# Four batches, all first-layer weights and two second-layer loads in transfers of 2 MB

## The chip, the cores and the metric

One core of a Trainium2 chip runs the whole kernel. The metric is the device time of one execution in microseconds (us). TensorE (PE) multiplies, VectorE (DVE), ScalarE (ACT) and GpSimd (POOL) do the rest, and SyncE (SP) issues nearly all transfers between HBM and on-chip memory. A transfer is cut into packets, one for each row that is contiguous on both sides, and they are spread over the core's 16 DMA engines. In this text 1 MB of a transfer is 1024 KB, that is 128 partitions of 8 KB.

## The reference

The inputs are `x` (8 batches, 8 heads, 512 tokens, 64), `state` (8, 8, 32, 64), and a soft mixture of 8 experts with 4 slots each (`phi`, `w1` 8x512x1024, `w2` 8x1024x512), all float32:

```
scores = x @ state.T / 8 ; a = softmax(scores) ; xread = a @ state
scores2 = state @ x.T / 8 ; a2 = softmax(scores2) ; sread = a2 @ x
X = concat(xread, sread) per batch, heads side by side      # 4608 x 512
logits = X @ phi
slot_input = softmax(logits, over tokens).T @ X             # 32 x 512
h = relu(slot_input[e] @ w1[e]) ; slot_out[e] = h @ w2[e]   # 4 slots of each expert
out = softmax(logits, over slots) @ slot_out                # 4608 x 512
```

Softmax denominators have 1e-9 added. The inputs are 8 MB of `x`, 0.5 MB of `state`, 16 MB of `w1` and 16 MB of `w2`; the output is 8.5 MB.

## The kernel before

The kernel has three stages. The first (to about 76 us) works through the 8 batches of attention and builds the logits and slot inputs; the order of its steps is written out by hand in the table `ORDER` (L30). The second runs the first layer: `w1_part(hf, e)` multiplies the slot inputs with half `hf` of expert `e`'s `w1`, 16 parts in all, from 76.2 us. The third runs the second layer over `w2` in column blocks (256 columns as `wide_part`, then twice 128 as `w2_part`), forms the outputs between them, and writes each block as it is done (`out`, `out_by_batches`, `out_st`). The order on every engine is the order in which the code is written.

All weights and batches pass through two pools of on-chip memory that go round: `big`, 13 buffers of 8 KB per partition, and `pairs`, 4 buffers of 16 KB (L76, L77). The 8 batches take the first 8 of `big`. The list `todo` (L105) is the order in which weights are loaded, and `load_w(n)` (L111) issues the next n of them on SP. The first 8 halves of `w1` go in twos into a buffer of `pairs`, but each by its own transfer of 1 MB; the other 8 and most of the first 256 columns of `w2` go to `big`, also 1 MB each; the remaining columns of `w2` (`w2b`) go as four transfers of 2 MB into `pairs`. Two experts' pieces of `w2` are loaded in smaller parts (`load_part`, L139) into memory that the attention stage gives back.

When a load is issued is set by when its buffer is free. At the start 13 loads are issued behind the batches (L676). After the second half of step `R` of each batch (L353), its last reader, that batch's buffer goes to the next load; after parts (0,1) and (0,3) of the first layer, one load each, and after (1,0) three more (L707 to L710). SP issues in order, and a transfer also waits until the eighth one before it has landed, since eight semaphores are used in turn. The output blocks are gathered in `big` (L806, L816).

Of the kernel before, what the change touches and what calls it, by code (L numbers as in the profile page):

```python
# [8 lines left out]
F32 = mybir.dt.float32  # L9
# [6 lines left out]
P = 128  # L16
B = 8
S = 512
NS = 32
D = 64  # L20
E = 8
F = 1024
NJ = S // P
EPS = 1e-9
NBIG = 13
NPAIR = 4
NH = 11


# [31 lines left out]


@with_exitstack
def attention_soft_moe(ctx: ExitStack, tc: tile.TileContext, x0, x1, x, st0, st1, phi, w1, w2a, w2b, out_x, out_s):

# [5 lines left out]
    nc = tc.nc  # L71
# [10 lines left out]
    phi_sb = cp.tile([P, 4, NS], F32, name="phi_sb")  # L82
    xb = []
    for b in range(B):
        t = big.tile([P, 4, NJ, 2 * D], F32, tag="big", name=f"x{b}")
        if b == 0:
            for i in range(4):
                v = x0[i].rearrange("p (g j c) -> p g j c", g=1, j=NJ)
                (act if i % 2 else nc.sync).dma_start(t[:, 1 * i : 1 * i + 1], v)
        elif b == 1:  # L90
            for i in range(2):
                v = x1[i].rearrange("p (g j c) -> p g j c", g=2, j=NJ)
                nc.sync.dma_start(t[:, 2 * i : 2 * i + 2], v)
        else:
            nc.sync.dma_start(t, x[b - 2].rearrange("p (g j c) -> p g j c", g=4, j=NJ))
        xb.append(t)
        if b == 0:
            nc.sync.dma_start(stT_sb[:, 0:1], st0)
        if b == 1:
            nc.sync.dma_start(stT_sb[:, 1:4], st1)  # L100
            nc.sync.dma_start(phi_sb, phi)


    w1t, w2t = {}, {}
    todo = [(1, hf, e) for hf in range(2) for e in range(E)]  # L105
    todo += [(2, k, e) for k in range(2) for e in range(0, E, 2)]
    last = todo.pop()
    todo += [(3, 0, 0), (3, 0, 4), last, (3, 1, 0), (3, 1, 4)]
    both = []

    def load_w(n):  # L111
        for _ in range(min(n, len(todo))):
            layer, k, e = todo.pop(0)
            if layer == 3:
                t = pairs.tile([P, 4 * F], F32, tag="pair", name=f"w3_{k}_{e}")
                t = t.rearrange("p (e k f) -> p e k f", e=4, k=8)
                nc.sync.dma_start(t, w2b[e // 4, k])
                for i in range(32):
                    w2t[3, k, e + i // 8, i % 8] = t[:, i // 8, i % 8]
                continue  # L120
            if layer == 1 and len(w1t) < 8 * NPAIR:
                if not both:
                    t = pairs.tile([P, 4 * F], F32, tag="pair", name=f"w1_{k}_{e}")
                    both.extend((t[:, 0 : 2 * F], t[:, 2 * F :]))
                t = both.pop(0)
            else:
                t = big.tile([P, 2 * F], F32, tag="big", name=f"w{layer}_{k}_{e}")
            if layer == 1:
                t = t.rearrange("p (k f) -> p k f", k=4)
                nc.sync.dma_start(t, w1[k, e])  # L130
                for i in range(4):
                    w1t[k, e, i] = t[:, i]
            else:
                t = t.rearrange("p (e k f) -> p e k f", e=2, k=4)
                nc.sync.dma_start(t, w2a[e // 2, k])
                for i in range(8):
                    w2t[layer, k, e + i // 4, i % 4] = t[:, i // 4, i % 4]

    def load_part(t, k, e, ft):  # L139
        n = t.shape[1] // 256  # L140
# [36 lines left out]
    with ExitStack() as actx:  # L177
# [162 lines left out]
        def R_(b, h):  # L340
            r = R[b]
            if h == 0:
                r["srp"] = mtile([P, 2, D], f"sr_ps{b}")
            for j in range(NJ):
                for g in range(4):
                    pe.matmul(  # L346
                        r["srp"][32 * g : 32 * g + 32, h, :],
                        r[f"eT{h}"][:, j, 32 * g : 32 * g + 32],
                        xb[b][:, g, j, D * h : D * h + D],
                        start=(j == 0),  # L350
                        stop=(j == NJ - 1),
                    )
            if h == 1:  # L353
                load_w(1)

        def sr(b):
# [308 lines left out]
        def SIe():  # L665
# [5 lines left out]
            E=E_, ee=ee, A=A_, ae=ae, R=R_, sr=sr, srT=srT, srTe=srTe, Lx=Lx, keep=keep, mx=mx, mk=mk,  # L671
            pv=pv, bm=bm, nme=nme, al=al, dx=dx, Lu=Lu, dT=dT, dTe=dTe, T=T_, tt=tt, U=U, Ue=Ue, Px=Px, Y=Y,
            Ls=Ls, Lse=Lse, Lr=Lr, msx=msx, als=als, dsx=dsx, Lus=Lus, lkp=lkp, D=Dn, V=V, Ve=Ve, Ps=Ps, Ys=Ys,
            xd=xd, ed=ed, ad=ad, srTd=srTd, Wd=Wd, We=We, Yf=Yf, SI=SI, SIe=SIe, windows=windows, mkd=mkd, W=warm, keepd=keepd, dTd=dTd, Ud=Ud, Vd=Vd,
        )
        load_w(NBIG - B + 2 * NPAIR)  # L676
        order = ORDER.split()

        states_read = max(order.index(f"S.{B - 1}"), order.index("U.1"))
        halves_had = max(order.index(t) for t in order if t.split(".")[0] in ("q", "aT", "e2", "ee", "ed", "windows"))  # L680
        (k1, e1), (k2, e2) = [todo.pop(B)[1:] for _ in range(2)]
        for i, step in enumerate(order):
            name, *args = step.split(".")
            steps[name](*map(int, args))
# [13 lines left out]
        def w1_part(hf, e):  # L698
            for kt in range(4):
                pe.matmul(  # L700
                    h_ps[hf][32 * kt : 32 * kt + 32, :],
                    si_m[kt // 2][:, 256 * (kt % 2) + 32 * e : 256 * (kt % 2) + 32 * e + 32],
                    w1t[hf, e, kt],
                    start=(e == 0),
                    stop=(e == E - 1),
                )
            if (hf, e) in ((0, 1), (0, 3)):  # L707
                load_w(1)
            if (hf, e) == (1, 0):
                load_w(3)  # L710

        def h_copy(hf):
            h_sb[hf] = half(f"h_sb{hf}")
# [19 lines left out]
        c = [half(f"c{i}") for i in range(3)]  # L733
        c = [v[:, 0 : t.shape[1]].rearrange("p (t n) -> p t n", n=NS) for v, t in zip(c, c_t)]
# [49 lines left out]
        def so_sum(k, half_of=0):  # L784
# [5 lines left out]
                so_r[i // 2] = half(f"so_r{i // 2}")[:, 0:256]  # L790
            act.copy(so_r[i // 2][:, P * (i % 2) : P * (i % 2) + P], p)

        def out(k, q):
            hf, col = k // 2, 128 * (k % 2)
            o = [(ps_t if j % 2 else ps_m).tile([P, 512], F32, tag="tr" if j % 2 else "ms", name=f"o{k}_{q}_{j}")
                 for j in range(NJ)]
            for j in range(NJ):
                rows = slice(32 * j, 32 * j + 32)
                pe.matmul(  # L799
                    o[j],  # L800
                    so_r[hf][rows, col : col + 128],
                    lt_all[rows, 4 * q : 4 * q + 4, :].rearrange("p b s -> p (b s)"),
                    start=True,
                    stop=True,
                )
            ot = big.tile([P, NJ, 512], F32, tag="big", name=f"out{k}_{q}")  # L806
            for jp in range(2):
                act.copy(ot[:, 2 * jp, :], o[2 * jp])  # L808
                dve.tensor_copy(ot[:, 2 * jp + 1, :], o[2 * jp + 1])  # L809
            nc.sync.dma_start(out_x[k, q], ot)  # L810

        def out_by_batches(k, q):
            hf, col = k // 2, 128 * (k % 2)
            homes = ((ps_m, "ms"), (ps_t, "tr"), (ps_m, "ms"), (ps_t, "tr"), (ps_s, "sc"), (ps_t, "tr"), (ps_s, "sc"), (ps_m, "ms"))
            o = [h.tile([P, 256], F32, tag=tag, name=f"o{k}_{q}_{i}") for i, (h, tag) in enumerate(homes)]
            ot = big.tile([P, 2, NJ, 256], F32, tag="big", name=f"out{k}_{q}")  # L816
            to = out_x[k, q].rearrange("p j s -> (p j s)").rearrange("(i p j s) -> i p j s", i=2, p=P, j=NJ)
            for i in range(2):
                b = 4 * q + 2 * i
                for j in range(NJ):  # L820
                    rows = slice(32 * j, 32 * j + 32)
                    pe.matmul(
                        o[4 * i + j],
                        so_r[hf][rows, col : col + 128],
                        lt_all[rows, b : b + 2, :].rearrange("p b s -> p (b s)"),
                        start=True,
                        stop=True,
                    )
# [119 lines left out]
```

## Time and profile before

| | |
|---|---|
| device time, median of 3 runs | 130.01 us (129.84 to 130.21) |
| span of the profiled execution, first to last instruction | 128.2 us |
| TensorE busy | 117.7 us, 92% of the span |
| VectorE, ScalarE, GpSimd busy | 68%, 60%, 35% |
| moved by DMA | 51.74 MB, mean 404 GB/s; SP's queue q1 takes 95.5% of 16 engines' span |
| HBM read, written | 42.53 MB, 8.91 MB |

The profile is that of one execution. Of its own it tells the span; what lies around the span is the difference between the time of a run and 128.2 us, 1.8 us against the median. Busy shares are means over the span, and a row of 40 digits shows them slice by slice (3.2 us each, 9 is 90% or more). "To landing" of a transfer is the time from its issue on SP until all of its 16 engines have reported. It holds the waiting behind earlier transfers too.

### The profile page before, as it was taken

To read this page: it belongs to the slowest core of one execution; us is meant where nothing else is said; L and a number is where in the kernel's file an instruction comes from. 1 tells how busy PE (TensorE), PEld (TensorE's weight loads), DVE (VectorE), ACT (ScalarE), POOL (GpSimd) and SP (SyncE) were. 2 spreads that over 40 slices of the span, in tenths; PEclk is the share of its full clock that TensorE was granted. 3 is DMA by queue.
4 is the path that set the end of the run, shared out by engine and by line. 5 is a ranking of instruction groups with operands and counts; after the bars stand their busy time and mean duration, and the time that the engine had idled before them with its cause. 6 is when DMAs were issued, how large, how long until landed. Compare 5 with 4: busy or idle time off the path is not lost.

```text
span 128.2 us, 4700 instructions
## 1 busy us (share of the span) xinstructions
PE 117.7 (92%) x1992; PEld 81.7 (64%) x1992; DVE 86.7 (68%) x194; ACT 76.9 (60%) x189; POOL 44.8 (35%) x63
## 2 busy tenths in 40 slices
PE   5999999999999999999999999999999999998600
PEld 2857686789795869768767769953465655575200
DVE  2329999999999999999985669019830356442600
ACT  4039999999999999999965711310100436645600
POOL 3004366391947467467882105703500000000000
PEclk9999999999999999999999999999999999999965
DMA  4999999999999999999999999999999989999992
GB/s 125 377 407 430 424 427 422 424 422 424 422 419 422 427 419 429 419 429 417 429 417 435 412 420 402 459 440 409 412 445 445 389 366 417 429 406 422 385 423 100
DMA packets 8373, 51.74 MB, mean 404 GB/s; under 512 B 928, under 2 KB 1184, under 8 KB 3360
## 3 DMA queue, kind: packets, MB, share of 16 engines
q1 hardware_dynamic: 8064, 50.93, 95.5%
q10 hardware_dynamic: 288, 0.52, 1.1%
q8 instruction: 15, 0.25, 0.7%
q14 instruction: 6, 0.05, 0.1%
HBM read 42.53 MB, written 8.91 MB: 401 GB/s over the span
## 4 chain that ended last, share of the span: by engine, by line
PE 71%; DVE 9%; DMA 7%; ACT 5%; issue 1%; POOL 0%; ACTq 0%; DVEq 0%; POOLq 0%
PE so_ps L763 12%; PE h_ps L700 11%; PE xt_ps L229 8%; PE o L799 7%; PE sc L248 5%; DMA phi_sb<-phi_in 5%; PE eT_ps L312 4%; PE sr_ps L346 4%; PE an_ps L312 3%; PE lt L381 3%; DMA x<-x_in 3%; PE t_ps L506 2%; DVE sums L277 2%; DVE q L261 2%; DVE m L266 1%
## 5 line engine op out<-in xcount | busy, mean ns | idle before, releaser
L270 POOL TENSOR_TENSOR q<-q,m 128x512 f32<-128x512 f32 x16 | 16.8, 1050 | 15.7 <-DVE m L266 7.3
L234 ACT ACTIVATE xt<-xt_ps 128x512 f32<-128x512 f32 x30 | 17.9, 618 | 5.9 <-PE xt_ps L229 5.7
L229 PE MATMUL xt_ps<-ident,x 128*128 128x128 f32 x128 | 19.3, 293 | 0.0
L288 POOL TENSOR_TENSOR q<-q,rr 128x512 f32<-128x512 f32 x16 | 16.5, 1051 | 5.1 <-DVE rr L283 3.6
L229 PEld LDWEIGHTS xt_ps<-ident,x 128*128 128x128 f32 x128 | 15.5, 151 | 3.1 <-PE sc L248 0.8
L763 PE MATMUL so_ps<-w,h_m 128*32 128x128 f32 (+1 forms) x384 | 15.7, 310 | 0.0
L763 PEld LDWEIGHTS so_ps<-w,h_m 128*32 128x32 f32 x384 | 10.7, 110 | 7.4 <-issue 4.6
L809 DVE COPY out<-o 128x512 f32<-128x512 f32 x14 | 9.2, 688 | 9.0 <-PE o L799 8.8
L700 PE MATMUL h_ps<-w,si_m 128*32 128x512 f32 x128 | 14.4, 594 | 0.1
L299 DVE TENSOR_REDUCE nm<-sc 128x1 f32<-128x512 f32 x16 | 10.6, 670 | 2.7 <-PE sc L248 2.7
L808 ACT COPY out<-o 128x512 f32<-128x512 f32 x14 | 7.7, 588 | 6.8 <-PE o L799 6.7
L700 PEld LDWEIGHTS h_ps<-w,si_m 128*32 128x32 f32 x128 | 9.1, 110 | 3.9 <-issue 2.9
L304 ACT ACTIVATE e<-sc,nm 128x512 f32<-128x512 f32 x16 | 11.3, 711 | 0.4 <-DVE nm L299 0.3
L261 DVE STREAM_TRANSPOSE q<-sc 128x512 f32<-128x512 f32 x16 | 11.1, 695 | 0.1
L293 DVE STREAM_TRANSPOSE aT<-q 128x512 f32<-128x512 f32 x16 | 10.9, 689 | 0.3 <-POOL q L288 0.2
L266 DVE TENSOR_REDUCE m<-q 128x16 f32<-128x512 f32 x16 | 10.5, 659 | 0.0
L277 DVE TENSOR_REDUCE sums<-q 128x16 f32<-128x512 f32 x16 | 10.4, 664 | 0.1
L273 ACT ACTIVATE q<-q 128x512 f32<-128x512 f32 x16 | 10.4, 650 | 0.1
L346 PE MATMUL sr_ps<-x,eT 128*32 128x64 f32 x512 | 10.4, 220 | 0.0
L312 PE MATMUL eT_ps<-ident,e 128*128 128x128 f32 x64 | 9.8, 279 | 0.0
L248 PE MATMUL sc<-xt,stT_sb 64*32 64x512 f32 x128 | 9.8, 601 | 0.0
L346 PEld LDWEIGHTS sr_ps<-x,eT 128*32 128x32 f32 x512 | 8.6, 110 | 1.3 <-issue 0.8
(124 smaller groups left out, 186.1 us busy)
## 6 DMA issues: line engine op xcount, KB each, us to landing
w<-w_in SPq DMA_DIRECT2D x16, 1024.0 KB, 19.7
w<-w2b_in SPq DMA_DIRECT2D x4, 2048.0 KB, 14.7
out_x<-out SPq DMA_DIRECT2D x7, 1024.0 KB, 6.0
x<-x_in SPq DMA_DIRECT2D x6, 1024.0 KB, 13.5
w<-w2a_in SPq DMA_DIRECT2D x6, 1024.0 KB, 19.4
x<-x_in SPq DMA_DIRECT2D x2, 512.0 KB, 5.9
w<-w2a_in SPq DMA_DIRECT2D x2, 512.0 KB, 12.4
w<-w2a_in SPq DMA_DIRECT2D x4, 256.0 KB, 14.4
```

The source lines that it names most:

```text
L229: pe.transpose(p[:, P * j : P * j + P], xb[b][:, g, j, :], ident)
L234: act.mul(r[f"xt{g}"], r[f"xp{g}"], 0.125)
L248: pe.matmul(r[f"sp{h}"][32 * g : 32 * g + 32, :], st_t(b, g)[64 * h : 64 * h + 64, :], r[f"xt{g}"][64 * h : 64 * h + 64, :], start=True, s ...
L261: dve.transpose(r[f"q{h}"], r[f"sp{h}"])
L266: dve.tensor_reduce(out=r[f"m1{h}"], in_=r[f"qv{h}"], axis=AX.X, op=ALU.max)
L270: pool.tensor_tensor(v, v, R[b][f"m1{h}"].broadcast_to([P, 16, NS]), op=ALU.subtract)
L277: dve.tensor_reduce(out=v, in_=R[b][f"qv{h}"], axis=AX.X, op=ALU.add)
L288: pool.tensor_tensor(v, v, r.broadcast_to([P, 16, NS]), op=ALU.mult)
L312: pe.transpose(p[:, j, :], r[f"{src}{h}"][:, P * j : P * j + P], ident)
L346: pe.matmul(r["srp"][32 * g : 32 * g + 32, h, :], r[f"eT{h}"][:, j, 32 * g : 32 * g + 32], xb[b][:, g, j, D * h : D * h + D], start=(j == ...
L700: pe.matmul(h_ps[hf][32 * kt : 32 * kt + 32, :], si_m[kt // 2][:, 256 * (kt % 2) + 32 * e : 256 * (kt % 2) + 32 * e + 32], w1t[hf, e, kt], ...
L763: pe.matmul(so[k][32 * i : 32 * i + 32, :], h_m[hf][:, 256 * i + 32 * e : 256 * i + 32 * e + 32], w(i), start=(hf == 0 and e == 0), stop=( ...
```

## The change

The two pools change sizes: `big` has 3 buffers of 8 KB, `pairs` 9 of 16 KB. The total stays at 168 KB per partition.

- Two batches share a buffer of `pairs`. Batches 0 to 3 are still loaded as before; 4 with 5 and 6 with 7 come as one transfer of 2 MB each.
- All of `w1` comes as eight transfers of 2 MB, two experts each, in place of sixteen of 1 MB.
- Of the 256-column pieces of `w2`, (0, 6) and (1, 0) come as one transfer of 2 MB (`w2c`); (0, 0), (0, 2) and (0, 4) take the three buffers of `big` and are issued at the start; (1, 6) takes half of a buffer of `pairs`.
- Since a buffer now holds two batches, loads are issued after step `R` of batches 1, 3, 5 and 6 only. After the first-layer part (1,0) two loads are issued in place of three, and one more after (1,1).
- Two output blocks share a buffer of `pairs`, still written by one transfer each.

On the host the arrays are laid out so that each of the merged transfers has rows of 16 KB that are contiguous in HBM.

```diff
-NBIG = 13
-NPAIR = 4
+NBIG = 3
+NPAIR = 9
...
     for b in range(B):
-        t = big.tile([P, 4, NJ, 2 * D], F32, tag="big", name=f"x{b}")
+        if b % 2 == 0:
+            two = pairs.tile([P, 2, 4, NJ, 2 * D], F32, tag="pair", name=f"x{b}")
+        t = two[:, b % 2]
...
-        else:
-            nc.sync.dma_start(t, x[b - 2].rearrange("p (g j c) -> p g j c", g=4, j=NJ))
+        elif b < 4:
+            nc.sync.dma_start(t, x2[b - 2].rearrange("p (g j c) -> p g j c", g=4, j=NJ))
+        elif b % 2:
+            nc.sync.dma_start(two, x[b // 2 - 2].rearrange("p (b g j c) -> p b g j c", b=2, g=4, j=NJ))
...
-    todo = [(1, hf, e) for hf in range(2) for e in range(E)]
-    todo += [(2, k, e) for k in range(2) for e in range(0, E, 2)]
-    last = todo.pop()
-    todo += [(3, 0, 0), (3, 0, 4), last, (3, 1, 0), (3, 1, 4)]
-    both = []
+    todo = [(1, hf, e) for hf in range(2) for e in range(0, E, 2)]
+    todo[5:5] = [(2, 0, 0), (2, 0, 2), (2, 0, 4)]
+    todo += [(4, 0, 0), (3, 0, 0), (3, 0, 4), (2, 1, 6), (3, 1, 0), (3, 1, 4)]
...
+            if layer == 2 and k == 0:
+                t = big.tile([P, 2 * F], F32, tag="big", name=f"w2_{k}_{e}")
+            else:
+                t = pairs.tile([P, 4 * F], F32, tag="pair", name=f"w{layer}_{k}_{e}")
...
+            elif layer == 1:
+                t = t.rearrange("p (e k f) -> p e k f", e=2, k=4)
+                nc.sync.dma_start(t, w1[k, e // 2])
...
+            elif layer == 4:
+                t = t.rearrange("p (n e k f) -> p n e k f", n=2, e=2, k=4)
+                nc.sync.dma_start(t, w2c)
...
-            if h == 1:
+            if (b, h) in ((1, 1), (3, 1), (5, 1), (6, 1)):
                 load_w(1)
...
-        load_w(NBIG - B + 2 * NPAIR)
+        load_w(NPAIR - B // 2 + NBIG)
...
-            if (hf, e) in ((0, 1), (0, 3)):
+            if (hf, e) in ((0, 1), (0, 3), (1, 1)):
                 load_w(1)
             if (hf, e) == (1, 0):
-                load_w(3)
+                load_w(2)
...
-            ot = big.tile([P, NJ, 512], F32, tag="big", name=f"out{k}_{q}")
+            if not homes_of_out:
+                t = pairs.tile([P, 2, NJ, 512], F32, tag="pair", name=f"out{k}_{q}")
+                homes_of_out.extend((t[:, 0], t[:, 1]))
+            ot = homes_of_out.pop(0)
```

The instructions of TensorE, VectorE, ScalarE and GpSimd stay the same in kind and order; the transfers on SP change. First, on SP from the fifth batch to the end of the loads issued at the start, before and then after (`x` are batches, `w_0_2` is a weight buffer of half or block 0 from expert 2, and the size is that of one transfer, 2048 elements being 8 KB a row):

```order
L95 DMA x_86<-x_in 128x2048
L95 DMA x_88<-x_in 128x2048
L95 DMA x_90<-x_in 128x2048
L95 DMA x_92<-x_in 128x2048
L130 DMA w_0_0_135<-w_in 128x2048 x2
L130 DMA w_0_2_138<-w_in 128x2048 x2
L130 DMA w_0_4_141<-w_in 128x2048 x2
L130 DMA w_0_6_144<-w_in 128x2048 x2
L130 DMA w_1_0_147<-w_in 128x2048
L130 DMA w_1_1_149<-w_in 128x2048
L130 DMA w_1_2_151<-w_in 128x2048
L130 DMA w_1_3_153<-w_in 128x2048
```

```order
L99 DMA x_84<-x_in 128x4096
L99 DMA x_86<-x_in 128x4096
L127 DMA w_0_0_129<-w_in 128x4096
L127 DMA w_0_2_131<-w_in 128x4096
L127 DMA w_0_4_133<-w_in 128x4096
L127 DMA w_0_6_135<-w_in 128x4096
L127 DMA w_1_0_137<-w_in 128x4096
L138 DMA w_0_0_139<-w2a_in 128x2048
L138 DMA w_0_2_141<-w2a_in 128x2048
L138 DMA w_0_4_143<-w2a_in 128x2048
```

Two transfers of 1 MB have become one of 2 MB, and three pieces of `w2` now stand ahead of the second half of `w1`.

Next, on SP, the loads that wait until a batch's buffer is free, before and then after:

```order
L130 DMA w_1_5_374<-w_in 128x2048
L130 DMA w_1_6_508<-w_in 128x2048
L130 DMA w_1_7_651<-w_in 128x2048
L135 DMA w_0_0_816<-w2a_in 128x2048
L135 DMA w_0_2_957<-w2a_in 128x2048
L135 DMA w_0_4_1128<-w2a_in 128x2048
L135 DMA w_0_6_1284<-w2a_in 128x2048
L135 DMA w_1_0_1410<-w2a_in 128x2048
```

```order
L138 DMA w_0_4_143<-w2a_in 128x2048
L127 DMA w_1_2_494<-w_in 128x4096
L127 DMA w_1_4_800<-w_in 128x4096
L127 DMA w_1_6_1110<-w_in 128x4096
L132 DMA w_0_0_1390<-w2c_in 128x4096
L145 DMA w_1_2_1400<-w2a_in 128x1024
```

Eight loads, each behind one batch, have become four, each behind two; the last of them still waits for the last step `R`.

Last, on SP, the end of the loads and the first outputs, before and then after:

```order
L142 DMA w_1_5_1661<-w2a_in 128x1024
L117 DMA w_0_0_1692<-w2b_in 128x4096
L117 DMA w_0_4_1702<-w2b_in 128x4096
L135 DMA w_1_6_1729<-w2a_in 128x2048
L117 DMA w_1_0_1731<-w2b_in 128x4096
L117 DMA w_1_4_1733<-w2b_in 128x4096
L810 DMA out_x<-out_0_1894 128x2048
```

```order
L145 DMA w_1_5_1641<-w2a_in 128x1024
L122 DMA w_0_0_1672<-w2b_in 128x4096
L122 DMA w_0_4_1682<-w2b_in 128x4096
L138 DMA w_1_6_1709<-w2a_in 128x2048
L122 DMA w_1_0_1711<-w2b_in 128x4096
L122 DMA w_1_4_1717<-w2b_in 128x4096
L818 DMA out_x<-out_0_1874 128x2048 x2
```

The order here is the same; only the buffers that these loads wait for are others.

## Rows read from the trace of the kernel before

**Rows 1.** The page: span, and the DMA engines' share in 40 slices

```profile
span 128.2 us, 4700 instructions
...
DMA  4999999999999999999999999999999989999992
```

**Rows 2.** The page, DMA queues: packets, MB, share of 16 engines

```profile
q1 hardware_dynamic: 8064, 50.93, 95.5%
...
q8 instruction: 15, 0.25, 0.7%
```

**Rows 3.** Waits of TensorE, the longest: us in total, times, longest us

```profile
PE warm_ps L649 <- POOL ident masks.py:199: 1.4, 1, 1.4
```

**Rows 4.** Waits of SP's queue from 120 us to the end

```profile
SPq L940 <- DMA out_x<-out: 5.4, 1, 5.4
```

**Rows 5.** Issues on SP from 118 to 123 us: start, duration, instruction

```profile
118.86 0.97 SPq L833 DMA_DIRECT2D out_x<-out  x2
119.92 0.52 SPq L851 DMA_DIRECT2D out_s<-out_s  x1
121.44 0.33 SPq L810 DMA_DIRECT2D out_x<-out  x1
```

**Rows 6.** Line 833 from 118 to 119.2 us: landing of its first transfer

```profile
DMA to landing us min/median/max: 4.0/4.0/4.0
```

**Rows 7.** Stretches: busy us and count by engine, PE clock, DMA share, GB/s

```profile
1.50:2.00 0.50, 0.50 (x1) 0.36 (x2) 0.47 (x4) 0.35 (x1) 0.20 (x1) 1.00 0.63 82
...
119.00:120.00 1.00, 1.00 (x7) 0.30 (x4) 0.56 (x3) 0.67 (x3) 0.00 (x0) 1.00 0.71 295
...
126.00:127.00 1.00, 0.00 (x0) 0.00 (x0) 0.00 (x0) 0.00 (x0) 0.00 (x0) 0.50 0.10 41
```

**Rows 8.** Line 130: all issues; landing of the first, then of the last

```profile
L130 SPq DMA_DIRECT2D w<-w_in x16: 327/328/429, 9.9 to 45.4; - x16
...
DMA to landing us min/median/max: 18.2/18.2/18.2
...
DMA to landing us min/median/max: 19.7/19.7/19.7
```

**Rows 9.** Line 142, its last part; line 117, its last two loads

```profile
L142 SPq DMA_DIRECT2D w<-w2a_in x1: 328/328/328, 74.9 to 74.9; - x1
...
DMA to landing us min/median/max: 8.8/8.8/8.8
...
L117 SPq DMA_DIRECT2D w<-w2b_in x2: 422/422/423, 84.8 to 85.3; - x2
DMA to landing us min/median/max: 16.2/18.3/20.4
```

**Rows 10.** Line 135: all issues; landings of the first, fifth and last

```profile
L135 SPq DMA_DIRECT2D w<-w2a_in x6: 328/328/328, 47.9 to 84.4; - x6
...
DMA to landing us min/median/max: 20.9/20.9/20.9
...
63.16 0.33 SPq L135 DMA_DIRECT2D w<-w2a_in  x1
...
DMA to landing us min/median/max: 15.4/15.4/15.4
...
DMA to landing us min/median/max: 11.4/11.4/11.4
```

**Rows 11.** Line 95, batches 4 and 5; then TensorE's first use of batch 4

```profile
L95 SPq DMA_DIRECT2D x<-x_in x2: 328/378/429, 5.8 to 6.4; - x2
DMA to landing us min/median/max: 12.6/13.5/14.4
...
24.48 0.60 PE L229 MATMUL xt_ps<-ident,x 128*128 128x128 f32 x4
```

**Rows 12.** TensorE on line 763 from 96 to 99.2 us

```profile
95.78 3.21 PE L763 MATMUL so_ps<-w,h_m 128*32 128x256 f32 x60
```

**Rows 13.** SP's issue of the first load of line 117

```profile
78.43 0.33 SPq L117 DMA_DIRECT2D w<-w2b_in  x1
```

More of the change, by code (lines that the diff above doesn't have):

```diff
@@ L63, in attention_soft_moe @@
 @with_exitstack
-def attention_soft_moe(ctx: ExitStack, tc: tile.TileContext, x0, x1, x, st0, st1, phi, w1, w2a, w2b, out_x, out_s):
+def attention_soft_moe(ctx: ExitStack, tc: tile.TileContext, x0, x1, x2, x, st0, st1, phi, w1, w2a, w2c, w2b, out_x, out_s):
     nc = tc.nc
@@ L113, in load_w @@
             layer, k, e = todo.pop(0)
+            if layer == 2 and k == 0:
+                t = big.tile([P, 2 * F], F32, tag="big", name=f"w2_{k}_{e}")
+            else:
+                t = pairs.tile([P, 4 * F], F32, tag="pair", name=f"w{layer}_{k}_{e}")
             if layer == 3:
-                t = pairs.tile([P, 4 * F], F32, tag="pair", name=f"w3_{k}_{e}")
                 t = t.rearrange("p (e k f) -> p e k f", e=4, k=8)
@@ L119, in load_w @@
                     w2t[3, k, e + i // 8, i % 8] = t[:, i // 8, i % 8]
[L120 to L125, printed above, removed]
-            else:
[L127 to L134, printed above, removed]
+            elif layer == 1:
+                t = t.rearrange("p (e k f) -> p e k f", e=2, k=4)
+                nc.sync.dma_start(t, w1[k, e // 2])
+                for i in range(8):
+                    w1t[k, e + i // 4, i % 4] = t[:, i // 4, i % 4]
+            elif layer == 4:
+                t = t.rearrange("p (n e k f) -> p n e k f", n=2, e=2, k=4)
+                nc.sync.dma_start(t, w2c)
+                for i in range(8):
+                    w2t[2, 0, 6 + i // 4, i % 4] = t[:, 0, i // 4, i % 4]
+                    w2t[2, 1, i // 4, i % 4] = t[:, 1, i // 4, i % 4]
+            else:
+                t = t[:, 0 : 2 * F].rearrange("p (e k f) -> p e k f", e=2, k=4)
                 nc.sync.dma_start(t, w2a[e // 2, k])
                 for i in range(8):
-                    w2t[layer, k, e + i // 4, i % 4] = t[:, i // 4, i % 4]
+                    w2t[2, k, e + i // 4, i % 4] = t[:, i // 4, i % 4]
     def load_part(t, k, e, ft):
@@ L680, in attention_soft_moe @@
         halves_had = max(order.index(t) for t in order if t.split(".")[0] in ("q", "aT", "e2", "ee", "ed", "windows"))
-        (k1, e1), (k2, e2) = [todo.pop(B)[1:] for _ in range(2)]
+        (k1, e1), (k2, e2) = (1, 2), (1, 4)
         for i, step in enumerate(order):
@@ L791, in so_sum @@
             act.copy(so_r[i // 2][:, P * (i % 2) : P * (i % 2) + P], p)
+        homes_of_out = []
         def out(k, q):
@@ L815, in out_by_batches @@
             o = [h.tile([P, 256], F32, tag=tag, name=f"o{k}_{q}_{i}") for i, (h, tag) in enumerate(homes)]
-            ot = big.tile([P, 2, NJ, 256], F32, tag="big", name=f"out{k}_{q}")
+            ot = big.tile([P, 2 * F], F32, tag="big", name=f"out{k}_{q}").rearrange("p (i j s) -> p i j s", i=2, j=NJ)
             to = out_x[k, q].rearrange("p j s -> (p j s)").rearrange("(i p j s) -> i p j s", i=2, p=P, j=NJ)
@@ L927 @@
         "x1_in": con(xl[1].reshape(P, 2, -1).transpose(1, 0, 2)),
-        "x_in": con(xl[2:]),
+        "x2_in": con(xl[2:4]),
+        "x_in": con(xl[4:].reshape(2, 2, P, -1).transpose(0, 2, 1, 3)).reshape(2, P, -1),
         "st0_in": con(sl[:, 0:1]),
@@ L931 @@
         "phi_in": con(moe_phi.reshape(4, 2, D, NS).transpose(1, 2, 0, 3)).reshape(P, 4, NS),
-        "w1_in": con(moe_w1.reshape(E, 4, P, 2, 512).transpose(3, 0, 2, 1, 4)),
-        "w2a_in": con(moe_w2[:, :, :256].reshape(E // 2, 2, 2, 4, P, 256).transpose(0, 2, 4, 1, 3, 5)),
+        "w1_in": con(moe_w1.reshape(E // 2, 2, 4, P, 2, 512).transpose(4, 0, 3, 1, 2, 5)),
+        "w2a_in": (wa := con(moe_w2[:, :, :256].reshape(E // 2, 2, 2, 4, P, 256).transpose(0, 2, 4, 1, 3, 5))),
+        "w2c_in": con(_np.stack([wa[3, 0], wa[0, 1]], axis=1)),
         "w2b_in": con(moe_w2[:, :, 256:].reshape(E // 4, 4, 8, P, 2, P).transpose(0, 4, 3, 1, 2, 5)),
```

## The prediction

> **What bounds the kernel now.** I read the page's head and slices first, then the waits of TensorE and of SP, then single transfers on SP by issue and landing. The reader should see two things that are both nearly full. The DMA engines' digit is 9 in every slice but the first and two of the last ones [rows 1], and SP's queue alone takes 95.5% of their span [rows 2]. TensorE, on the other side, never waits long for anything: its longest wait is 1.4 us at the very start, for the identity matrix [rows 3]. So up to the last output the arithmetic sets the pace of the issues, and the queue follows closely behind.
>
> What ends last is a transfer: SP waits 5.4 us for the last output [rows 4]. That output is issued at 121.4 and the waiting ends at about 127.2. 1 MB takes 2.47 us (below), and an idle queue moves its first data at most 1.3 us after the first issue at 0.7 (nothing before 1.5, share 0.63 from 1.5 to 2.0 [rows 7]). Alone, that output would have landed by 121.4 + 1.3 + 2.5 = 125.2. So some 2.0 us at the end are waiting in line. The line is not equal for all 16 engines: from 119 to 120 us their share is only 0.71, so many had run dry, and from 126 to 127 it is 0.10, so one or two work alone [rows 7]. A transfer has landed when its slowest engine reports, so the end belongs to the engine that is furthest behind. For that engine, I now ask whether it was ever idle. The first half of the output before it is issued at 118.9 [rows 5] and lands 4.0 us later, at 122.9 [rows 6]; its 0.5 MB take 1.2 us, so its turn came at 121.6, 1.4 us after the latest moment at which its data could have gone (118.9 + 1.3 = 120.2). There the slowest engine had work on hand with 1.4 us to spare. Any time saved in its line, up to 1.4 us, therefore reaches the end.
>
> **The price of a packet.** The line is bytes plus a price per packet. For rows of 8 KB: the first load of line 130 lands at 9.9 + 18.2 = 28.1 and the sixteenth at 45.4 + 19.7 = 65.1 [rows 8], so 15 MB take 37.0 us, 2.47 us for each MB. For rows of 16 KB: the last small part lands at 74.9 + 8.8 = 83.7 and the last `w2b` load at 85.3 + 20.4 = 105.7 [rows 9]. In these 22.0 us go four transfers of 2 MB and one of 1 MB with rows of 8 KB (line 135, 84.4 us [rows 10]): (22.0 - 2.47) / 8 = 2.44 us for each MB. Each engine gets 1/16 of the 128 rows of 1 MB, so 8 packets of 8 KB or 4 of 16 KB. Four packets fewer save 0.026 us, 6.5 ns for one. A third point: the six parts between the load issued at 63.2, which lands at 63.2 + 15.4 = 78.6 [rows 10], and 83.7 are 2 MB, half in rows of 4 KB and half in rows of 2 KB, 24 packets an engine and MB on the mean; 5.1 / 2 = 2.55 us a MB, and (2.55 - 2.47) / 16 gives 5 ns. Landings are read to 0.1 us, so the first estimate may be anything from 3 to 10 ns. I take 6.5 ns, since it comes from the same two sizes of rows that the change trades.
>
> **What is removed.** Merged are one pair of `x` transfers twice (4 MB), all of `w1` (16 MB) and the pair of `w2` pieces (2 MB): 22 MB. That is 22 x 4 = 88 packets fewer on each engine: 88 x 6.5 ns = 0.57 us, from 88 x 3 = 0.26 to 88 x 10 = 0.88. The price of a completion report is inside it, since it was measured between whole transfers. SP issues 11 transfers fewer of 0.33 us, which is worth nothing: in the loads it stood waiting for earlier landings (issues up to 20.9 us ahead of them [rows 10]).
>
> Here a rule of the Trainium skill says much more. In "SBUF — State Buffer", section "The DMA setup-cost knee (why "@ 1 MiB" ≠ asymptote)", every transfer pays some 2 us that do not grow with its size, and it advises the largest single transfers. By that rule 11 transfers fewer would be an estimated 22 us, and the end would fall back to what the arithmetic allows. The rows don't agree: transfers of 1 MB land 2.47 us apart, so whatever setup they have lies beside the data of those ahead.
>
> **What is moved, and its cover.** I cost these at nothing, each with the work that hides it.
> - Batch 4 lands with batch 5 in place of 2.4 us earlier. Batch 5 lands at 6.4 + 14.4 = 20.8, and TensorE first uses batch 4 at 24.5 [rows 11]: 3.7 us of cover. Batch 6 with 7 has more, since it is used later still.
> - Loads now wait for two batches. The last of them still waits for the same step `R` as the load at 63.2 before. With it the line then reached to 78.6; the new load holds 2 MB, so the line ahead of it ends 2 MB earlier, at 73.7, still 10 us ahead. If that cover were gone, all engines would be dry, and each us of it would be a us at the end, or a late weight.
> - Three pieces of `w2` stand ahead of the second half of `w1`. The last of `w1` then lands where the third load of line 135 does now, 65.1 + 3.7 + 2 x 2.47 = 73.7, before the first layer begins at 76.2.
> - The `w2b` loads keep their order. The first waits for a buffer until part (0,1) as before, 78.4 [rows 13]; the line then holds work until 83.7, and 0.6 us less of it and 1.3 us for the way still leave more than 3. The last now waits until part (1,1), about 1 us later than before, but with 2 MB transfers ahead of it in a line that is some 15 us long.
> - The closest weight is (1, 6) of the 256 columns. It lands at 84.4 + 11.4 = 95.8 [rows 10]. Of the 60 matmuls from 95.8 on [rows 12], the last 24 are parts (1,6), (1,7) and the first narrow one, so its use begins 36/60 into 3.2 us, at 97.7: 1.9 us of cover, which grows with the saving.
> - The first output block waits for more semaphores, of transfers that landed long before.
>
> **Sum.** Span 128.2 - 0.57 = 127.6. With 1.8 us around the span, which I leave unchanged (median 130.0 against 128.2), 129.4 us.
>
> **Rivals.**
> 1. *The saving doesn't show.* The engine that is furthest behind has got there by jumps, not by packet prices: the last load of line 130 lands at 65.1, and the next, at 47.9 + 20.9 [rows 8, 10], at 68.8, 3.7 us later in place of 2.47, 1.2 us lost. The queue of instructions moves 15 packets of about 16 KB [rows 2], and one of 16 KB costs 2.44 / 4 = 0.61 us of one engine; two on the same engine in turn would make just such a jump. If the late engine in the new program gets one more of these, 0.57 - 0.61 gives 130.0; if the price of a packet is 3 ns, 129.7. For it: the saving is the size of one such packet. Against it: the four engines that compute run the same instructions in the same order, and fetch the same. The Trainium skill speaks for the small price: "DMA: Bandwidth & Descriptors", section "Why small descriptors are slow (HBM only)", gives a fixed overhead of about 3 cycles a packet, by its own clock of 850 MHz an estimated 3.5 ns, 0.31 us in all and 129.7. The rows at 5 and 6.5 ns are nearer to twice that.
> 2. *More than forecast.* If the jumps spread more evenly, the slowest engine falls in with the others, and the end is what the last issues allow: 2.0 us less, 128.0. For it: most engines do run dry at 119. Against it: nothing in the change spreads them.
> 3. *Slower.* The late engine, between 28 us and the first outputs, is hit by two more instruction packets than now (or by a wait of 1.2 us behind the longer data packets): 2 x 0.61 - 0.57 = 0.65 us more at the end, 130.7. It decides from two packets on, as one is balanced. For it: the jump of 1.2 us shows that an engine can lose two at once. Against it: the number of such packets hangs on the program's length, which falls by a few instructions on SP.
>
> **How the numbers follow.** Two measurements of this kernel differ by about 0.3%, 0.39 us, so less can't be told from no change. The forecast and what lies near it (129.0 to 129.6) gets 0.54, and rival 2 0.04; together 0.58 for faster. Rival 1 (129.7 to 130.3) gets 0.31, rival 3 0.11. The range runs from 128.8, the upper end of the packet price with a jump spread a little better, up to 130.2, into rival 1; left out are rival 2, rival 3 and the edge of rival 1. The likeliest case's own range is 129.1 to 129.75 (0.88 and 0.26 us).
>
> **What would show it.** Queue q1 has 8064 - 1408 data packets and 11 x 16 = 176 reports fewer, 6480. Loads of `w1` land 4.88 us apart, not 4.94. The issues of the last outputs stay at 118.9 and 121.4, TensorE has no new wait for a weight, and SP's last wait falls from 5.4 to about 4.8 us. I am wrong if the last issue moves, if TensorE waits for a weight or a batch, if a slice in the middle falls below 9 in the DMA row, or if the last landing stays at 127.2 with packets gone.

## The result, and the profile after

The changed kernel takes 130.93 us (median of 10 runs, 130.4 to 131.2) against 130.09 us before: ratio 1.0061 [1.0043, 1.0079]. It is slower, where 129.4 us was forecast, and lies outside the range. The runs of the experiments gave the unaltered changed kernel twice more, with 1.0040 and 1.0036. So the loss is 0.5 to 0.8 us. The profiled execution shown here took 130.40 us, the fastest of the ten, so that it shows 0.4 us of the loss. A few executions were in a slower state, two of `f0_again` and one of `f1_three` below; their medians hold them, the ratios leave them out.

The page of the changed kernel, its span, the DMA engines' slices and its queues (packets, MB, share of 16 engines), to lay beside [rows 1, 2]:

```profile
span 128.6 us, 4685 instructions
...
DMA  3999999999999999999999999999999979999990
...
q1 hardware_dynamic: 6480, 50.92, 94.6%
...
q8 instruction: 15, 0.25, 0.7%
```

The change did what it says: 6480 packets on q1, as forecast. The count of TensorE's instruction packets (q8) is the same. The slice from 102.9 to 106.1 us is now at 7; before, it had the row's one 8.

Next, single loads, to see whether the line of transfers got shorter. The load of before that ends the same work as the last `w1` load of after (third of line 135, issued at 52.9 us), issue and landing:

```profile
L135 SPq DMA_DIRECT2D w<-w2a_in x1: 328/328/328, 52.9 to 52.9; - x1
...
DMA to landing us min/median/max: 20.9/20.9/20.9
```

And of after: the last `w1` load (SP's timeline, then its landing), and the landing of the last `w2b` load, issued at 85.5:

```profile
51.76 0.33 SPq L127 DMA_DIRECT2D w<-w_in  x1
...
DMA to landing us min/median/max: 21.6/21.6/21.6
...
DMA to landing us min/median/max: 19.9/19.9/19.9
```

Before, this point of the line is reached at 52.9 + 20.9 = 73.8 us, after at 51.8 + 21.6 = 73.4. By then 20 MB have gone in long rows, 80 packets fewer on each engine: 0.4 / 80 = 5 ns a packet in this pair. The last `w2b` load lands at 105.4 in place of 105.7 [rows 9]. One pair is little, as a landing differs by up to 0.4 us between executions. Over the profiles of all runs below, this point is reached at 73.8 us on the mean of five executions with all these rows at 16 KB, and at 74.1 of seven with all at 8 KB; the last `w2b` load lands at 105.6 and 105.9. So there is a saving, 0.3 us or 4 ns a packet, and it is still there at 105 us.

Where it went is seen in the stretches (columns as in [rows 7]). Before:

```profile
103.00:104.00 1.00, 1.00 (x16) 0.24 (x15) 0.10 (x1) 0.14 (x1) 0.00 (x0) 1.00 0.73 287
```

After:

```profile
103.00:104.00 1.00, 1.00 (x12) 0.27 (x8) 0.14 (x1) 0.00 (x0) 0.00 (x0) 1.00 0.41 164
...
119.00:120.00 1.00, 1.00 (x8) 0.48 (x8) 0.68 (x3) 0.74 (x3) 0.00 (x0) 1.00 0.72 303
...
126.00:127.00 1.00, 0.00 (x0) 0.00 (x0) 0.00 (x0) 0.00 (x0) 0.00 (x0) 0.50 0.06 25
```

From 103 to 104 us the engines' share is 0.41 in place of 0.73: most of them are done with the loads earlier, and the outputs aren't there yet. At 119 and at 126 us all looks as before. SP's timeline tells why, first the early outputs of before, then of after:

```profile
102.96 7.01 SPq L810 DMA_DIRECT2D out_x<-out  x4
```

```profile
103.21 7.01 SPq L818 DMA_DIRECT2D out_x<-out  x4
...
119.08 1.00 SPq L841 DMA_DIRECT2D out_x<-out  x2
120.16 0.49 SPq L859 DMA_DIRECT2D out_s<-out_s  x1
121.69 0.33 SPq L818 DMA_DIRECT2D out_x<-out  x1
```

Every output is issued some 0.25 us later than before, from the first one on; the last at 121.69 in place of 121.44 [rows 5]. So the arithmetic is late. TensorE's waits of after name two places that have no other engine as their cause, and are longer than the 0.2 us that line 381, the same as 384 of after, shows before (first row):

```profile
PE lt L381 <- issue: 0.2, 1, 0.2
...
PE lt L384 <- issue: 0.4, 1, 0.4
...
PE sr_ps L349 <- issue: 0.3, 1, 0.3
```

One more difference stands at the very end, in SP's own instructions of the last line. Before (first all up to 127.42 us, then the DRAINs):

```profile
L940 SPq EVENT_SEMAPHORE  x4: 28/28/5343, 121.9 to 127.4; - x4
...
L940 SPq DRAIN  x3: 7/7/7, 127.4 to 127.7; - x3
```

After (the same two):

```profile
L950 SPq EVENT_SEMAPHORE  x2: 28/28/28, 127.2 to 127.3; - x2
...
L950 SPq DRAIN  x3: 7/7/129, 127.7 to 128.2; - x3
```

The columns are duration in ns (least, median, most) and the first and the last start. Before, SP goes from its last wait for an output straight into the DRAIN, both at 127.4. After, the wait is over at 127.3 and the DRAIN starts at 127.7. Nothing that the profile names lies in these 0.4 us, and the other engines wait for SP there. The last output itself has landed at the same time in both, 127.2: it took 5.5 us from its issue in place of 5.8. So in this pair of executions SP's 0.4 us are the whole difference of the spans.

So three things are to be explained: a saving that doesn't reach the end, outputs issued 0.25 us late, and 0.4 us on SP at the end.

### The profile page after: what moved, and what is told of

Read it like the earlier page. It is cut to its first block, busy times and chain, and to the rows that moved or that the text cites. A ratio compares the mean times of both kernels' runs of the same rounds, so it can differ in the third digit from the quotient of the medians.

```text
span 128.6 us, 4685 instructions
## 1 busy us (share of the span) xinstructions
PE 116.9 (91%) x1992; PEld 80.8 (63%) x1992; DVE 86.9 (68%) x194; ACT 76.9 (60%) x189; POOL 44.7 (35%) x63
## 3 DMA queue, kind: packets, MB, share of 16 engines
q1 hardware_dynamic: 6480, 50.92, 94.6%
## 4 chain that ended last, share of the span: by engine, by line
PE 71%; DVE 14%; DMA 7%; issue 2%; POOL 0%; ACT 0%; DVEq 0%; ACTq 0%; POOLq 0%
PE so_ps L766 12%; PE h_ps L703 11%; PE xt_ps L232 8%; PE o L804 7%; PE sc L251 5%; DMA phi_sb<-phi_in 4%; PE an_ps L315 4%; PE sr_ps L349 4%; PE eT_ps L315 4%; DMA x<-x_in 3%; PE lt L384 2%; DVE sums L280 2%; DVE q L264 2%; PE t_ps L509 2%; DVE aT L296 2%; DVE nm L302 2%
## 5 line engine op out<-in xcount | busy, mean ns | idle before, releaser
L232 PE MATMUL xt_ps<-ident,x 128*128 128x128 f32 x128 | 18.5, 284 | 0.0
L232 PEld LDWEIGHTS xt_ps<-ident,x 128*128 128x128 f32 x128 | 14.8, 146 | 3.3 <-ACT xt L237 0.8
L703 PE MATMUL h_ps<-w,si_m 128*32 128x512 f32 x128 | 14.4, 594 | 0.1
```

Source lines behind the costliest of these rows:

```text
L232: pe.transpose(p[:, P * j : P * j + P], xb[b][:, g, j, :], ident)
L703: pe.matmul(h_ps[hf][32 * kt : 32 * kt + 32, :], si_m[kt // 2][:, 256 * (kt % 2) + 32 * e : 256 * (kt % 2) + 32 * e + 32], w1t[hf, e, kt], ...
```

## The experiments

The theories, by the letters of the texts on record:

- **A, SP's program.** Instructions are fetched in blocks through the DMA engines. The change has 13 SP instructions fewer (84 in place of 97), so SP steps into a new block at another place: before, while it waited for the outputs anyway, after, at the last DRAIN.
- **D, TensorE's program.** TensorE's blocks come as packets of 16 KB through the same DMA engines as the weights. Data packets of 16 KB delay them, and TensorE waits for instructions, which its row of waits calls "issue".
- **E, a saving without use.** The queue runs dry before the outputs, so time saved before that is idle time there.

The rivals to A and D are the other parts of the change: the new order of the loads and the shared buffers.

Every ratio is to the kernel before on the same chip, with its 95% interval.

### SP's program (A)

The changed kernel again, unaltered, twice:

> The changed kernel once more, unaltered, for a second profile and as the standard on this chip. Every theory: 130.9 us (130.4 to 131.2). In its trace the last landing tells which part of the excess is before it (the queue) and which behind it (SP's end: 1.4 us from the last landing to the end in the first profile, 1.0 before the change).

> The changed kernel unaltered, as the standard beside the next three on one chip. All theories: 130.6 to 130.9 us, 0.4 us between SP's last wait and its drain, last issue at 121.7 or later.

Measured: 130.61 us, 1.0040 [1.0018, 1.0062], and 130.75 us, 1.0036 [1.0007, 1.0064]. The loss is real. Then the changed kernel with empty instructions on SP behind the loads of the start:

```diff
         load_w(NPAIR - B // 2 + NBIG)
+        for i in range(13):      # e1_nops; 3 in f1_three
+            nc.sync.nop(f"pad{i}")
```

> The changed kernel with 13 empty instructions on SP behind the loads issued at the start, so that SP's later instructions stand again at the places in its program that they had before the change. Theory A (SP's program crosses into a new block of code at a fixed count of instructions; the change has 13 fewer and so moves that crossing from among the last outputs, where SP waits anyway, to the very end, where 0.4 us of it shows): 130.5 us, 0.4 less than the changed kernel, the gap behind the last wait gone. Theory B (the excess lies in the transfers: 16 KB packets hold up instruction fetches or the slowest DMA engine): no change, 130.9. Theory C (order of loads and coarser buffers): no change.

> The changed kernel with 3 empty instructions on SP in place of 13: the crossing then falls three instructions ahead of the drain, among the waits for the last landings, where SP stands anyway. Theory A: the gap of 0.4 us is gone and the time falls by 0.4, to 130.2 to 130.5. Rival (the 13 instructions helped by delaying SP's issues at the start): no gain, 130.6 to 130.9.

Measured: with 13, 130.28 us, 0.9993 [0.9975, 1.0011]; with 3, 130.31 us, 0.9997 [0.9966, 1.0028]. Adding work that does nothing takes away some 0.4 us; 13 against none is clear of the noise, 3 against none overlaps. And the other way round, the kernel before with 115 empty instructions (with blocks of 128, 115 more is the same place in a block as 13 fewer):

```diff
         load_w(NBIG - B + 2 * NPAIR)
+        for i in range(115):
+            nc.sync.nop(f"pad{i}")
```

> The kernel before with 115 empty instructions on SP behind the loads issued at the start, which cost SP about 2 us where it waits for landings. If a block of code is 128 instructions, the next crossing then falls where it does in the changed kernel, on the last drain. Theory A: 130.5 us, 0.4 more than the kernel before, with the gap of 0.4 us behind SP's last wait. Theories B and C: 130.1, no change.

Measured: 130.45 us, 1.0016 [1.0001, 1.0032]: slower. Its trace has the gap at the end, which the kernel before has not (the last line, as above):

```profile
L942 SPq EVENT_SEMAPHORE  x4: 28/28/5572, 121.7 to 127.4; - x4
...
L942 SPq DRAIN  x3: 7/7/130, 127.8 to 128.2; - x3
```

The gap goes with the count of SP's instructions and with nothing else of the change: of all sixteen profiles, those with 84 instructions on SP (four) or 212, which is 84 + 128 (`e2_before_nops`), have 0.35 to 0.43 us between the last wait and the DRAIN, the eleven others, with 87 to 98, have 0.04. The trace's packet records agree: the last instruction packet of 8 KB (q14) moves with SP's count. It starts at 119.9 us before and 120.9 in `e1_nops`, where SP had outputs still to wait for, but at 128.4 in after and 128.5 in `e2_before_nops`. A holds: the step into a new block costs 0.4 us where it falls on the last DRAIN, about half of the loss. In the five profiles with the gap the packet starts 0.6 to 0.9 us after the DRAIN, so SP didn't wait for this packet's data; what it does in the gap no row shows.

The Trainium skill has a rule on it: "Runtime: NRT & Kernel Launch", section "Instruction fetch mechanics", says that the sequencer fetches the next block of the program by its own DMA queue, in blocks of 16 KiB, and that the cost of crossing is mostly hidden. The traces agree on such a queue for TensorE (q8, packets of 16 KB). They differ on the rest: SP's packet is 8 KB and comes on q14, with five more whose times don't move with SP's count, and at the last DRAIN 0.4 us were in the open.

### The rows of 16 KB (D)

The changed kernel with its buffers, its order and its layout, but each merged transfer issued as two of 1 MB, so with rows of 8 KB and with 11 transfers more on SP; then the same with 2 empty instructions:

```diff
-                nc.sync.dma_start(t, w1[k, e // 2])
+                for i in range(2):
+                    nc.sync.dma_start(t[:, i], w1[k, e // 2][:, i])
```

(and so for `x` and `w2c`)

> The changed kernel's buffers and order, but each merged transfer issued as two of 1 MB with rows of 8 KB (11 transfers more; SP has 97 instructions, 2 fewer than before the change, so its crossing falls among the last outputs). Theory A: 130.1 to 130.5 (no gap at the end; without the packets' saving). Theory B: 130.1, as before the change, since the long packets are gone. Theory C: 130.9, since order and buffers are still there. If 16 KB packets save what was predicted, this is 0.5 us slower than e1.

> The merged transfers issued as two of 1 MB again, with 2 empty instructions so that SP has as many as before the change. Theory D (packets of 16 KB hold up TensorE's instruction fetches): last issue 121.2 to 121.5, no or at most 0.2 us of issue wait on TensorE, 130.05. Rival (packets don't matter at all): as f3 and as the changed kernel with 13 empty instructions, 130.3.

Measured: 130.05 us, 0.9991 [0.9971, 1.0010], and 130.16 us, 1.0009 [0.9985, 1.0032]. As fast as before: the order of the loads and the shared buffers cost nothing that could be measured, nor does the layout in HBM, which is that of the changed kernel here. It falls to the transfers themselves, their number (A) and their rows.

Next, which rows. `e4_late` merges only three loads of the second half of `w1`, (1,2), (1,4) and (1,6); `e5_early` the two `x` pairs, three early loads of `w1` and `w2c`. The others are split as above; 5 and 8 empty instructions keep SP's count.

> The changed kernel's buffers and order with only three loads merged, the first-layer loads (1,2), (1,4), (1,6), which move from about 57 to 73 us; the others go as two of 1 MB with 8 KB rows; 5 empty instructions on SP keep its crossing among the last outputs. Theory D (TensorE's own instruction blocks are fetched through the same DMA engines, and 16 KB data packets ahead of them make them come later than needed where its instructions are short, at about 37, 62 and 68 us): TensorE waits 0.4 to 0.8 us for nothing else on the lt line at 68, not at 37, and the last issue is 0.3 to 0.7 us later than in e3_split; time 130.2 to 130.5. Rival (the wait at 68 us is chance, or comes from the order of loads): no such wait, as in e3_split, 130.05.

> The changed kernel with the loads that move from 30 to 40 and from 57 to 73 us split in two (first-layer (0,2), (0,4), (1,2), (1,4), (1,6)); both batch pairs, three first-layer loads and the pair of second-layer pieces stay merged; 8 empty instructions on SP. Theory D: no issue wait on TensorE at 37, 62 or 68 us, last issue as in e3_split (121.2), and six merged loads save 0.3 us of the queue; time 129.8 to 130.05, the least of all if the queue's saving reaches the end at all. Rival: the waits stay, 130.3.

Measured: 130.06 us, 1.0009 [0.9989, 1.0029], and 129.99 us, 0.9989 [0.9971, 1.0008]. D had forecast a longer wait of TensorE near 68 us for `e4_late`; it was no longer than in the kernel before (0.35 against 0.45 us, table below). In this form D missed: long rows that move only near the wait don't bring it out, and about half of them cost nothing that could be measured. The time of `e5_early` is as D had it, but not each sign: its last output is issued at 121.39, and TensorE's weight loads wait 0.3 us near 37 us.

The clean test of the rows keeps the transfers of 2 MB, their number and their order, and changes only the layout in HBM, so that a row is 8 KB:

```diff
-                nc.sync.dma_start(t, w1[k, e // 2])
+                nc.sync.dma_start(t, w1[k, e // 2].rearrange("e p k f -> p e k f"))
...
-        "w1_in": con(moe_w1.reshape(E // 2, 2, 4, P, 2, 512).transpose(4, 0, 3, 1, 2, 5)),
+        "w1_in": con(moe_w1.reshape(E // 2, 2, 4, P, 2, 512).transpose(4, 0, 1, 3, 2, 5)),
```

(and so for `x` and `w2c`) With 13 empty instructions:

> The changed kernel with 13 empty instructions on SP and all merged transfers of 2 MB kept, but their data laid out in HBM so that each row is 8 KB: the number of packets is that before the change, the number and order of transfers that after it. Beside e1_nops it differs in the row length alone. Theory D: as f2_split13, no more than 0.2 us of issue wait on TensorE, last issue 121.2 to 121.5, 130.05, 0.2 less than e1_nops. The prediction's packet price: 0.57 us more than e1_nops, 130.85. Theory E (the queue's time doesn't count): no more than 0.1 us from f2.

Measured: 129.70 us, 0.9980 [0.9950, 1.0010], the lowest so far, and below what D had forecast. To settle both causes, three kernels on one chip: this one again, without the empty instructions, and the long rows with them.

> The changed kernel with both costs taken away: 2 MB transfers, but rows of 8 KB (other layout in HBM), and 13 empty instructions on SP. Two causes (SP's crossing 0.3 to 0.4 us, long rows 0.2 to 0.3): at or below the kernel before, 129.6 to 130.1, ratio 0.996 to 1.000; no 'issue' wait of TensorE above 0.3 us, last output issued at about 121. Only the crossing: the same as the changed kernel with 13 empty instructions beside it.

> The same without the 13 empty instructions: long rows undone, crossing kept. Two causes: 0.3 to 0.4 us above the run with them, 130.0 to 130.4, with the gap of 0.4 us before SP's last DRAIN back. If the crossing only matters together with late outputs: equal to the run with them. If all of the slowdown were the crossing: as slow as the changed kernel, 130.6 to 130.9.

> The changed kernel with rows of 16 KB and 13 empty instructions on SP: crossing undone, long rows kept. Two causes: 0.2 to 0.4 us above the run with rows of 8 KB and the same 13 (so 130.1 to 130.4), with 0.4 us or more of 'issue' wait of TensorE near 68 us and the last output issued after 121.7. Only the crossing: equal to that run within 0.1 us.

| ratio to before | SP short, as changed | SP padded |
|---|---|---|
| rows of 16 KB | 1.0061, 1.0040, 1.0036 | 0.9993, 0.9997, 1.0018 [0.9989, 1.0047] (`g3_nops`, 130.39 us) |
| 2 MB, rows of 8 KB | 1.0012 [1.0000, 1.0024] (`g2_rows8_bare`, 130.16 us) | 0.9980, 0.9981 [0.9969, 0.9993] (`g1_rows8`, 129.87 us) |

Both causes show, and as far as the noise tells they add. For SP's block `g1_rows8` against `g2_rows8_bare` doesn't overlap. For the rows no pair on one chip is clear of the noise by itself (`g1_rows8` against `g3_nops` overlaps by a hair), but all go the same way. With the means of the four fields the rows cost 0.4 us (by an estimate from the intervals, 0.2 to 0.5) and SP's block 0.5 us (0.3 to 0.6). `g1_rows8` is faster than the kernel before. Its end, and that of `g2_rows8_bare`:

```profile
L952 SPq EVENT_SEMAPHORE  x2: 28/28/28, 126.9 to 127.0; - x2
...
L952 SPq DRAIN  x3: 7/7/7, 127.0 to 127.4; - x3
```

```profile
L950 SPq EVENT_SEMAPHORE  x2: 28/28/28, 126.9 to 127.0; - x2
...
L950 SPq DRAIN  x3: 7/7/116, 127.4 to 127.9; - x3
```

Both are through with the wait for their last output at 127.0, and have the DRAIN at 127.0 and at 127.4.

One expectation failed: `g3_nops` should have had the wait near 68 us and a late last output. It had neither in its profile, an execution of 129.44 us, the fastest of its 12 runs (up to 131.06). (The profile of `e1_nops` is the slowest of its 12, 130.91 us.) That leads to how D works. TensorE's weight loads of line 384 at about 68 us (start, duration, and the idle time before, in brackets), in `g1_rows8`, after, `e1_nops` and `g3_nops`:

```profile
67.82 0.16 PEld L384 LDWEIGHTS lt<-aT,G_sb 128*32 128x32 f32 x8 [0.16 <-issue]
```

```profile
68.35 0.16 PEld L384 LDWEIGHTS lt<-aT,G_sb 128*32 128x32 f32 x8 [0.65 <-issue]
```

```profile
69.02 0.16 PEld L384 LDWEIGHTS lt<-aT,G_sb 128*32 128x32 f32 x8 [1.10 <-issue]
```

```profile
67.48 0.16 PEld L384 LDWEIGHTS lt<-aT,G_sb 128*32 128x32 f32 x8 [0.16 <-issue]
```

Beside them, from the packet records, the end of TensorE's instruction packet (16 KB, queue q8), and SP's last output issue:

| | rows | packet ends | weights start | idle before | last issue |
|---|---|---|---|---|---|
| `f3_rows8` | 8 KB | 66.31 | 67.61 | 0.16 | 120.92 |
| `g1_rows8` | 8 KB | 66.43 | 67.82 | 0.16 | 121.13 |
| `e3_split` | 8 KB | 66.37 | 67.77 | 0.18 | 121.17 |
| `f2_split13` | 8 KB | 66.25 | 67.78 | 0.43 | 121.17 |
| `g2_rows8_bare` | 8 KB | 66.67 | 68.08 | 0.43 | 121.39 |
| before | 8 KB | 66.68 | 68.03 | 0.45 | 121.44 |
| `e2_before_nops` | 8 KB | 66.49 | 67.83 | 0.41 | 121.22 |
| `e6_less` (below) | 8 KB | 66.82 | 68.27 | 0.37 | 121.67 |
| `e4_late` | some 16 KB | 66.67 | 68.03 | 0.35 | 121.43 |
| after | 16 KB | 66.95 | 68.35 | 0.65 | 121.69 |
| `e0_same` | 16 KB | 67.18 | 68.53 | 0.82 | 121.86 |
| `f1_three` | 16 KB | 67.06 | 68.54 | 0.82 | 121.87 |
| `e1_nops` | 16 KB | 67.62 | 69.02 | 1.10 | 122.45 |
| `g3_nops` | 16 KB | 66.13 | 67.48 | 0.16 | 120.80 |

In all fourteen the weights start 1.30 to 1.53 us after the packet has ended, wherever it ends between 66.1 and 67.6: TensorE waits here for its instructions, also in the kernel before. The last output follows 53.3 to 53.4 us later in all fourteen. (In `e5_early` TensorE came to this place 0.4 us late by itself and didn't wait there. The profile of `f0_again` is left out, as that execution is 1.2 us late from its first 11 us on; it has the same 1.5 and 53.4 us.)

That the wait is one for the packet is borne out by its places: in `e1_nops` the waits near 37, 62 and 68 us come before TensorE's 1219th, 2243rd and 2498th matmul or weight load, 1024 and 255 apart (a record can be missing), and there are 15 packets for some 4020 of them. So one half of D is shown: TensorE waits for this packet, and what it waits more here is late at the end. The other half, that long rows make the packet late, is shown in part. With all rows at 16 KB in four executions of five it came later than in any other of the table, and in the fifth it did not. Of after's 0.3 us against before at this place, 0.2 are the longer wait, and TensorE brought 0.1 with it. The first of the 15 packets is a further hint: in the nine with no long rows among the early loads it starts at 14.4 to 15.1 us, in the five and `e5_early` at 15.1 to 15.5, though TensorE is no later there than in the nine by more than 0.2. The size of the effect is that of the table of ratios. Why `g3_nops` and `e5_early` have made it up by 66 us stays open.

### A saving without use (E)

The kernel before with one load of 1 MB left out, the second half of expert 7 in the first layer, for which expert 6's weights are used, and 2 empty instructions:

```diff
+            if (layer, k, e) == (1, 1, 7):
+                for i in range(4):
+                    w1t[1, 7, i] = w1t[1, 6, i]
+                continue
```

> The kernel before with one first-layer load of 1 MB left out (expert 7's second half is multiplied with expert 6's weights), so 2.47 us less in the queue, and nothing else changed but 2 empty instructions on SP. The prediction's reading (the engine that is furthest behind is never idle before the end, so what is saved in the line reaches the end up to 1.4 us): 128.7 us. Theory E (most engines run dry at 103 us, when the loads are over and the first outputs not yet issued; from there the end is set by the issues of the outputs and by instruction fetches that fall on an engine behind that): 129.6 to 130.0, under 0.5 us gained.

Measured: 129.97 us, 0.9995 [0.9976, 1.0015]. 2.47 us of the line were taken away, and the time stood still. Its stretches, its last `w2b` load and its last issue:

```profile
80.00:81.00 1.00, 1.00 (x15) 0.94 (x11) 0.16 (x1) 0.42 (x1) 1.00 (x2) 1.00 0.70 221
...
103.00:104.00 1.00, 1.00 (x10) 0.25 (x8) 0.13 (x1) 0.00 (x0) 0.00 (x0) 1.00 0.12 49
```

```profile
L121 SPq DMA_DIRECT2D w<-w2b_in x1: 328/328/328, 83.8 to 83.8; - x1
...
DMA to landing us min/median/max: 21.0/21.0/21.0
```

```profile
121.67 0.33 SPq L816 DMA_DIRECT2D out_x<-out  x1
```

The engines stand at 0.70 at 80 us, so part of the saving is lost there: the first `w2b` load lands at 86.6 in place of 88.6, 2.0 us earlier than before, the last, at 83.8 + 21.0 = 104.8, only 0.9 [rows 9]. At 103 us they stand at 0.12: most have nothing left. The first output is then issued 0.2 us later than before, at 103.2, and lands 0.4 later, at 109.2 in place of 108.8, so nothing is left of the 0.9 either. In all sixteen profiles the last output lands 5.5 to 6.1 us after its issue, whatever was saved earlier. E holds in its result: what is saved before the outputs doesn't reach the end. That the slowest engine, too, runs dry ahead of them is not shown.

## Why the prediction was wrong

**The step that failed first** is "Any time saved in its line, up to 1.4 us, therefore reaches the end." I had measured that the slowest engine had work on hand at 119 us, and concluded that it had been in arrears all along. `e6_less` refutes it: 2.47 us less in its line gave 0.06 us (0.9995), inside the interval. For most engines the line starts anew at 103 us, before the first output, and there I had read no stretch. The sign stood in [rows 1]: of what I called "two of the last ones", one is the slice from 102.6 to 105.8 us, an 8, just where the first output is issued. What makes one engine late at 119 us stays open. TensorE's 16 KB instruction packets at 104.0 and 114.2 us before, and 103.9 and 114.4 after, may do it; that was not tried by itself.

**The price of a packet** was about right: 5 ns in the pair shown and 4 ns as a mean over the profiles, against 6.5 and within 3 to 10. The Trainium skill's "DMA: Bandwidth & Descriptors", section "Why small descriptors are slow (HBM only)", with about 3 cycles a packet, an estimated 3.5 ns, comes as near.

**"SP issues 11 transfers fewer of 0.33 us, which is worth nothing"** failed on the other side. I looked for what SP gains, in its waits, and not for what moves when its program gets shorter: 0.4 us lost at the last DRAIN (A), with no data transfer involved.

**"The issues of the last outputs stay at 118.9 and 121.4"** failed: 119.08 and 121.69. I had named the sign, "I am wrong if the last issue moves", and had no price for it. The instructions on TensorE are the same in kind and order, but not the time at which they arrive (D). The row that shows it was in the waits of before, 0.2 us of "issue" on line 381; I gave it no price.

**Rival 3** had the place wrong and part of the cause right. It had instruction packets and "a wait of 1.2 us behind the longer data packets", but as a delay of the data of the engine that is late. The last output's data took no longer with long rows, 5.5 us from issue to landing in after against 5.8 before; it was a delay of the engine whose instructions the packets carry. Against it I wrote that the program's length "falls by a few instructions on SP", and it was these that made about half of the loss.

**What was moved** cost nothing that could be measured, as forecast: `e3_split`, with all moves and no merging, is at 0.9991 [0.9971, 1.0010].

**The sum by the runs.** With both costs taken away the change is worth -0.2 us (`g1_rows8`, 129.87 against 130.08); to it come 0.4 us for the rows and 0.5 for SP's block, which makes +0.7, against +0.5 to +0.8 measured. That is no check of its own, since the parts come from the same table. Where the 0.2 us come from was not tried; in the profile TensorE waits 0.16 in place of 0.45 us at 68 us, and the last output is issued 0.3 us earlier than before.

## What to carry to other kernels

A queue that is 95% full can still be idle at the one moment that matters: before a saving in it is counted, look in stretches of 1 us for the last place where most of it runs dry, and expect little from what is saved ahead of that. When a change alters the number of instructions on an engine, look at what that engine does last: the step into a new block of its program may fall there, and a few empty instructions, which here cost nothing that could be measured, show it. A wait with no cause but "issue" on the engine that sets the pace can be a load of its own, its program: the page lists those packets among the same 16 DMA engines as the data.

## What the runs showed of the hardware that was not expected

- Three empty instructions on SP made a kernel 0.4 us faster on the mean (`f1_three` against `f0_again`, 0.9997 against 1.0036, intervals that overlap; with 13, in `e1_nops`, they don't), and 115 made another 0.2 to 0.3 us slower (`e2_before_nops`): where SP's step into a new block of its program falls on the last DRAIN, 0.35 to 0.43 us pass there, in five profiles of five.
- TensorE started 1.3 to 1.5 us after its instruction packet had ended, in all of fourteen executions, with the packet's end anywhere from 66.1 to 67.6 us.
- Transfers of 2 MB with rows of 8 KB were better than the same transfers with rows of 16 KB: 129.87 against 130.39 us on one chip (the intervals just overlap), although 1408 packets more are moved.
